# When the first MLP's narrow units are mixed into attention: a delay of 6,500 instead of 13,000 and a reserve of 54,000 instead of 60,000

## The chip, the cores and the metric

One core of one Trainium2 chip. The metric is the device time of one execution in microseconds (us); lower is better. Engines are named as in the profile: PE (TensorE matmuls), PEld (its weight loads), DVE (VectorE), ACT (ScalarE), POOL (GpSimd), SP (the queue that issues the DMAs).

## What is computed

Attention with a memory term (4 batches, 8 heads, 576 tokens, 64 wide), then two MLPs over the 2,304 tokens, all in fp32:

```python
scores = scale * q @ k.T; scores = where(causal, -1e9, scores)
a = softmax(scores); local = a @ v
q_p = phi(q)                                   # elu(q) + 1
mem_out = (q_p @ M_prev) / (q_p . z_prev + 1e-6)
x = g * mem_out + (1 - g) * local              # (2304, 512)
h = x @ w_in;  x = elu(h) @ w_out              # first MLP, d_ff 2048
h = x @ w2_in; out = leaky(h) @ w2_out         # second MLP, d_ff 2048
```

## The kernel before

**Precision.** fp32 values are split into a high and a low part (`xh`, `xl`; `gh`, `gl`; two slices of each weight tile `w`), and a product is made of three matmuls. Batch 0 of attention alone runs in plain fp32.

**Attention** (`attention_units`, up to L591) runs over 16 pairs of heads, four per batch, each of four items. An item has stages that are woven together: scores and softmax (`score`, L428 to L451), transposes of the probabilities (`tr`, L457), and the product with the values (`pv`, L524 to L532), whose result goes to DRAM (`xq_scr`, L532).

**The first MLP** has two shapes. Its first 7 of 16 slices of d_ff are computed batch by batch as **narrow units** on half a batch (288 tokens): `u_load` (L670 to L676, two loads `x` and `y` of what attention wrote), `u_x` (L682 adds the two, L610 casts to `xh` on ACT, L614 makes `xl` on POOL, for four chunks c = 0 to 3), then seven `u_h` units (12 matmuls each, L621, then ACT L633 and L634, DVE L635, the cast L241 and POOL L628), then four `u_o` units (21 matmuls each, L649, a copy L241 to `st`, a store L703 to `ys`). A batch thus has 22 units and 336 narrow matmuls. The other 9 slices and the whole second MLP follow as wide work on 512 tokens, with PE's queue full to the end.

**The order around the change** is set by a planner (L752 to L779) whose costs are planned nanoseconds, not times of the chip. `c0` is attention up to the end of batch 0 (47,290), `c_att` the rest of it (130,950), `c_mlp` all narrow units (161,280). At each attention unit of cost `c` the first MLP earns `c * rate` of credit; a narrow unit is handed out when its credit is there and `pos` is at least `DELAY` past the end of its batch:

```python
rate = (c_mlp - RESERVE) / (c_att - DELAY)
fill += [(pos + DELAY, c2, u2) for c2, u2 in more]
if fill and fill[0][0] <= pos:
    credit += c * rate
while fill and fill[0][0] <= pos and fill[0][1] <= credit:
    _, c2, u2 = fill.pop(0)
```

What is left when attention ends (`side`) is then issued ahead of the wide work, with the decoding of six weight tiles mixed in (`merge`, `load_w`, L103 to L138). The framework's scheduler takes this order as priorities and may still move single instructions on each engine; each engine's queue is executed in order. From here on the first `u_x` of batch n is called the start of batch n.

Of the kernel before, what the change touches and what calls it, by code (L numbers as in the profile page):

```python
# [24 lines left out]
def kernel(  # L25
# [36 lines left out]
    NTT = NT // TN  # L62
    NG = 7
    DSPAN = 0.75
    RESERVE = 60000.0
    EARLY = 150
    DELAY = 13000.0
    NHP = H // 2
    PSUM = bass.MemoryType.PSUM

# [686 lines left out]
    c_mlp = NFA * 24 * NT / 2.4  # L757
    rate = (c_mlp - RESERVE) / (c_att - DELAY)
    dec = [lambda f=f: load_w(0, wpa, w1i, w1o, f, f) for f in range(NFA)]
    fill = []  # L760
    credit = pos = 0.0
    for c, u, done in att:
# [7 lines left out]
        if done is not None:  # L770
            fetch, more = phase1_units(done)
            fetch()
            fill += [(pos + DELAY, c2, u2) for c2, u2 in more]
        if fill and fill[0][0] <= pos:
# [188 lines left out]
```

## Time and profile before

| | us |
|---|---|
| median of 3 runs | 1075.36 (1072.89 to 1075.43) |
| the profiled execution's own time | 1075.3 |
| its span, first to last instruction | 1073.5 |
| PE busy / PEld busy in the span | 1042.7 / 911.4 |
| DVE / ACT / POOL busy | 595.5 / 483.5 / 532.4 |

The span is cut at the places that matter: batch 0 of attention ends near 88 us, narrow matmuls begin at 124.7 us, attention's last matmul is at 394 us, and from 426 us on PE's queue is full. "Busy" of PE counts a matmul's modelled length, which overlaps the next one.

### The profile page before, as it was taken

The numbers are of one execution on the slowest core, as the hardware profiler recorded it, in microseconds if no ns is written. First come the engines' busy times: TensorE is split into PE (matmuls) and PEld (weight loads), VectorE is DVE, ScalarE is ACT, GpSimd is POOL, SyncE is SP. The second block draws the span as 40 slices with busy tenths as digits, with TensorE's granted clock in tenths as the row PEclk, the third lists the DMA queues.
The fourth block names the chain that finished last, engine by engine and source line by source line (L and its number), as shares of the span: only waits on it lengthen the run. The fifth ranks groups of instructions, "written<-read, shape, count | busy, mean of one in ns | idle before, by whom it ended". The sixth has DMA issues, their size and how long they took to land.

```text
span 1073.5 us, 17323 instructions
## 1 busy us (share of the span) xinstructions
PE 1042.7 (97%) x5904; PEld 911.4 (85%) x5904; DVE 595.5 (55%) x1382; ACT 483.5 (45%) x1169; POOL 532.4 (50%) x674
## 2 busy tenths in 40 slices
PE   7998899999998999999999999999999999999997
PEld 4776799989998998988888889888888888888896
DVE  6889987788879748576762325654322221232232
ACT  6999887778877635544442224332211211110111
POOL 7675775667657626654543225855422422222221
PEclk9999999999999999999999999999999999999999
DMA  7754544564446238765562304430200100000010
GB/s 183 197 144 116 162 137 105 124 169 144 108 121 164 89 95 286 251 227 188 191 224 66 118 1 138 157 118 1 79 1 1 64 15 1 10 30 1 1 40 20
DMA packets 150408, 115.05 MB, mean 107 GB/s; under 512 B 80048, under 2 KB 142000, under 8 KB 150320
## 3 DMA queue, kind: packets, MB, share of 16 engines
q1 hardware_dynamic: 150320, 113.94, 35.6%
q8 instruction: 47, 0.77, 0.3%
q14 instruction: 41, 0.34, 0.1%
HBM read 78.52 MB, written 31.85 MB: 103 GB/s over the span
## 4 chain that ended last, share of the span: by engine, by line
PE 87%; DVE 6%; DMA 3%; issue 1%; ACT 1%; SPq 1%; POOL 0%; DVEq 0%; ACTq 0%; POOLq 0%
PE pm L621 20%; PE tp L621 16%; PE sc L911 14%; PE sc L649 10%; PE pm L649 4%; PE po L911 4%; PE po L524 4%; PE tp L457 4%; PE po L649 3%; PE pm L524 2%; PE sc L428 1%; PE sc L426 1%; PE sc L429 1%; DVE pt L431 1%; DMA y<-xq 1%
## 5 line engine op out<-in xcount | busy, mean ns | idle before, releaser
L628 POOL TENSOR_TENSOR gl<-e,gh 128x512 fp32r<-128x512 f32 (+2 forms) x181 | 202.8, 1123 | 378.0 <-DVE gh L243 266.4
L621 PE MATMUL tp<-xw,w 128*128 128x512 f32 (+1 forms) x504 | 144.0, 367 | 0.0
L621 PE MATMUL pm<-xw,w 128*128 128x512 f32 (+1 forms) x496 | 142.1, 369 | 0.0
L911 PE MATMUL sc<-w,gh 128*128 128x512 f32 x448 | 135.9, 390 | 0.0
L451 POOL TENSOR_SCALAR pt<-pt,rs,omg 128x128 f32<-128x128 f32 (+4 forms) x160 | 102.5, 649 | 22.9 <-DVE rs L446 18.2
L649 PE MATMUL sc<-gh,w 128*128 128x512 f32 (+2 forms) x438 | 105.4, 340 | 0.3 <-DVE gh L243 0.3
L621 PEld LDWEIGHTS tp<-xw,w 128*128 128x128 f32 x504 | 91.8, 189 | 16.1
L621 PEld LDWEIGHTS pm<-xw,w 128*128 128x128 f32 x496 | 90.6, 188 | 16.1
L436 ACT ACTIVATE pt<-pt,mx 128x128 f32<-128x128 f32 (+4 forms) x160 | 93.0, 583 | 16.6 <-DVE mx L431 15.7
L911 PEld LDWEIGHTS sc<-w,gh 128*128 128x128 f32 x448 | 83.1, 188 | 16.5
L621 PE MATMUL tp<-xv,w 128*128 128x512 f32 (+1 forms) x252 | 92.5, 367 | 0.0
L621 PE MATMUL pm<-xv,w 128*128 128x512 f32 (+1 forms) x248 | 91.4, 369 | 0.0
L640 ACT ACTIVATE e<-pm 128x512 f32<-128x512 f32 (+1 forms) x40 | 22.2, 554 | 145.2 <-PE pm L621 142.2
L138 POOL TENSOR_TENSOR w<-wm,w 128x512 fp32r<-128x512 f32 x50 | 65.8, 1337 | 37.9 <-ACT w L241 37.9
L641 DVE TENSOR_TENSOR e<-tp,e 128x512 f32<-128x512 f32 (+1 forms) x40 | 25.5, 636 | 106.2 <-ACT e L640 106.2
L911 PE MATMUL sc<-w,gl 128*128 128x512 f32 x224 | 84.3, 389 | 0.0
L243 DVE CAST gh<-e 128x512 fp32r<-128x512 f32 (+2 forms) x146 | 75.4, 520 | 13.8 <-PE po L911 3.1
L649 PEld LDWEIGHTS sc<-gh,w 128*128 128x128 f32 x438 | 74.9, 188 | 9.3 <-DVE gh L243 0.6
L621 PE MATMUL pm<-xh,w 128*128 128x288 f32 x368 | 81.3, 308 | 1.5 <-ACT xh L610 1.4
L457 PE MATMUL tp<-ident,pt 128*128 128x128 f32 x480 | 80.3, 276 | 2.3 <-ACT ah L247 0.8
L641 DVE TENSOR_TENSOR e<-pm,e 128x512 f32<-128x512 f32 (+1 forms) x40 | 25.4, 636 | 102.4 <-ACT e L640 102.4
L640 ACT ACTIVATE e<-tp 128x512 f32<-128x512 f32 (+1 forms) x40 | 22.1, 552 | 117.2 <-PE tp L621 117.2
(157 smaller groups left out, 2444.7 us busy)
## 6 DMA issues: line engine op xcount, KB each, us to landing
wraw<-in_moe_w_in_dram SPq DMA_DIRECT2D x32, 512.0 KB, 3.9
wraw<-in_moe_w_out_dram SPq DMA_DIRECT2D x32, 512.0 KB, 4.7
xh<-xh SPq DMA_DIRECT2D x8, 576.0 KB, 3.1
xl<-xl SPq DMA_DIRECT2D x8, 576.0 KB, 4.1
ys<-st SPq DMA_DIRECT2D x32, 144.0 KB, 2.8
x<-x1s SPq DMA_DIRECT2D x9, 512.0 KB, 3.8
out_dram<-st SPq DMA_DIRECT2D x36, 128.0 KB, 1.7
vn<-in_v_dram SPq DMA_DIRECT2D x64, 64.0 KB, 2.3
```

Of the source, the lines that this page charges most:

```text
L138: nc.gpsimd.tensor_tensor(out=w[:, 1, a], in0=t[:, a], in1=_f(w)[:, 0, a], op=ALU.subtract)
L243: (nc.vector if eng == "V" else nc.gpsimd).tensor_copy(dst, src)
L436: nc.scalar.activation(out=pt[0:m, 0:nk], in_=pt[0:m, 0:nk], func=AF.Exp, scale=-1.0, bias=mx[0:m, last:last + 1], accum_out=self.pd["ss"] ...
L451: nc.gpsimd.tensor_scalar(out=pt, in0=pt, scalar1=rs[0:m, i:i + 1], scalar2=omg[0:m, h:h + 1], op0=ALU.mult, op1=ALU.mult,)
L457: nc.tensor.transpose(dst, self.p[c][:, k0:k0 + kn], ident)
L524: nc.tensor.matmul(po[:, a:b], w, x, start=i == 0, stop=i == len(mms) - 1)
L621: nc.tensor.matmul(ph, wi[:, wj, kc, :], xx[:, kc, :], start=n_mm == 0, stop=n_mm == 11)
L628: nc.gpsimd.tensor_tensor(out=gl, in0=g, in1=_f(gh), op=ALU.subtract)
L640: nc.scalar.mul(t, ph, 0.01)
L641: nc.vector.tensor_tensor(out=t, in0=ph, in1=t, op=ALU.max)
L649: nc.tensor.matmul(py, wo[:, wj, ec * P:(ec + 1) * P], gg, start=opens and f == first and n_mm == 0, stop=closes and f == last and n_mm == 2,)
L911: nc.tensor.matmul(pos[tb], gg[:, tb * P:(tb + 1) * P], wo[:, wj, :], start=f == 0 and n_mm == 0, stop=f == NF - 1 and n_mm == 2,)
```

## The change

Two constants of the planner; nothing else:

```diff
-    RESERVE = 60000.0
+    RESERVE = 54000.0
     EARLY = 150
-    DELAY = 13000.0
+    DELAY = 6500.0
```

`rate` goes from 0.859 to 0.862. The condition on `DELAY` holds back batch 0 alone: batches 1 and 2 become due before the last unit of the batch ahead of them is handed out, with either value. 33 units (29 now) are left over when attention ends.

ACT, at the start of batch 0 (`xh` is its cast tile, L610; L436, L342 and L249 belong to attention):

```order
190 L249 CAST ac<-tp 64x320
191 L610 CAST xh_1825<-x 128x288 x3
192 L436 ACTIVATE pt_1664,ss_157<-pt_1664,mx 128x128
193 L342 CAST qs_1586<-sc 64x320
194 L249 CAST dh_137<-tp 128x384
195 L436 ACTIVATE pt_1677,ss_157<-pt_1677,mx 128x256
```

and in the changed kernel:

```order
190 L249 CAST ac<-tp 64x320
191 L610 CAST xh_1671<-x 128x288 x3
192 L436 ACTIVATE pt_1664,ss_157<-pt_1664,mx 128x128
193 L610 CAST xh_1671<-x 128x288
194 L342 CAST qs_1586<-sc 64x320
195 L249 CAST dh_137<-tp 128x384
```

Before, the fourth cast (which every `u_h` needs) stands 27 rows behind the first three; now one row behind them. PE follows: its first narrow matmul has 387 attention matmuls ahead of it, 469 before, and 72 narrow matmuls now stand ahead of the 470th attention matmul. PE's queue there, as a difference:

```order
 L428 MATMUL sc<-kk_1538,qs_1585 128x448
 L429 MATMUL sc<-kl_1_176,qs_1585 128x448
+L621 MATMUL pm<-xh_1671,w_201 128x288 x2
+L621 MATMUL pm<-xh_1671,w_391 128x288 x2
 L524 MATMUL po<-ac,vv 128x320
 L524 MATMUL po<-dh_153,vv 128x256
```

The rest of batch 0's first units follow some 30 attention matmuls later. The stretches without narrow matmuls between two batches change too, counted in attention matmuls on PE: between batches 0 and 1 from 59 to 47, between batches 1 and 2 from 39 to 78.

PE at the end of attention (L524 is its last matmul; `gh`, `gl` are batch 2's second half), changed kernel:

```order
2008 L524 MATMUL po<-dl_139,vv 128x128
2009 L649 MATMUL sc<-gl,w_905 128x288
2010 L649 MATMUL sc<-gh,w_1010 128x288 x2
...
2028 L649 MATMUL sc<-gh,w_1010 128x288 x2
2029 L649 MATMUL sc<-gl,w_1010 128x288
2030 L621 MATMUL tp<-xh_6579,w_201 128x288 x2
2031 L621 MATMUL pm<-xh_6579,w_391 128x288 x2
2032 L621 MATMUL tp<-xh_6579,w_539 128x288 x2
2033 L621 MATMUL pm<-xh_6579,w_650 128x288 x2
```

33 narrow matmuls now stand between attention's last matmul and the first of batch 3; before there were 73. The first four `u_h` of batch 3 now run side by side in all four banks of `tp` and `pm`; before it was two. On ACT all four `st` copies of batch 2's last half now stand ahead of batch 3's casts, two before; `st` has two buffers.

## Rows read from the trace of the kernel before

**Rows 1.** Page, part 1: busy us, share of the span, instructions.
```profile
PE 1042.7 (97%) x5904; PEld 911.4 (85%) x5904; DVE 595.5 (55%) x1382; ACT 483.5 (45%) x1169; POOL 532.4 (50%) x674
```
**Rows 2.** Windows: stretch, length, busy PE, PEld, DVE, ACT, POOL (instructions); clock, DMA share, GB/s.
```profile
109.50:124.70 15.20, 12.36 (x83) 9.53 (x82) 14.92 (x47) 11.81 (x34) 11.27 (x20) 1.00 0.44 110
124.70:200.00 75.30, 75.25 (x591) 74.74 (x590) 61.49 (x187) 60.19 (x173) 52.88 (x85) 1.00 0.51 138
200.00:240.00 40.00, 36.78 (x266) 34.69 (x264) 33.56 (x104) 30.35 (x87) 26.02 (x42) 0.96 0.61 161
240.00:304.00 64.00, 64.00 (x505) 63.67 (x504) 53.79 (x162) 51.63 (x148) 45.05 (x72) 1.00 0.50 129
304.00:350.00 46.00, 41.72 (x305) 39.73 (x304) 40.04 (x118) 35.20 (x101) 32.39 (x51) 0.96 0.52 137
...
394.40:404.10 9.70, 9.70 (x75) 9.70 (x75) 2.82 (x6) 1.87 (x5) 2.10 (x4) 1.00 0.69 191
404.10:426.00 21.90, 19.59 (x143) 18.83 (x142) 17.47 (x26) 13.20 (x26) 13.18 (x14) 1.00 0.97 327
```
**Rows 3.** Timeline of ACT, batch 0's casts: start, length, engine, line, what, count.
```profile
106.38 1.10 ACT L610 CAST xh<-x 128x288 fp32r<-128x288 f32 x3
...
123.67 0.44 ACT L610 CAST xh<-x 128x288 fp32r<-128x288 f32 x1
```
**Rows 4.** Timeline of PE: the first narrow matmuls.
```profile
124.68 0.75 PE L621 MATMUL pm<-xh,w 128*128 128x288 f32 x4
```
**Rows 5.** Timeline of PE at 387 us: nine narrow matmuls lie between these two starts.
```profile
387.13 0.43 PE L621 MATMUL tp<-xh,w 128*128 128x288 f32 x2
...
388.33 0.43 PE L621 MATMUL tp<-xh,w 128*128 128x288 f32 x2
```
**Rows 6.** Timeline of ACT and of DVE: what one narrow `u_h` costs there.
```profile
127.91 0.40 ACT L633 ACTIVATE e<-pm 128x288 f32<-128x288 f32 x1
...
129.13 0.45 ACT L634 ACTIVATE e<-e 128x288 f32<-128x288 f32 x1
...
129.98 0.42 ACT L241 CAST gh<-e 128x288 fp32r<-128x288 f32 x1
...
129.28 0.45 DVE L635 SCALAR_TENSOR_TENSOR e<-e,pm 128x288 f32<-128x288 f32 x1
```
**Rows 7.** Timeline of DVE, then of PE, around the two starts of batch 2.
```profile
303.36 1.20 DVE L682 TENSOR_TENSOR x<-x,y 128x288 f32<-128x288 f32 x3 [1.38 <-DMA vn<-in_v_dram]
...
344.31 0.41 PE L524 MATMUL po<-qph,ms 128*128 128x320 f32 x1 [1.92 <-DVE xp L531]
```
**Rows 8.** Windows, PE alone: stretch, length, busy, granted clock, DMA share, GB/s.
```profile
226.00:230.00 4.00, 4.00 (x21) 0.57 0.84 321
346.00:348.00 2.00, 2.00 (x11) 0.50 0.26 59
420.00:425.00 5.00, 2.69 (x17) 1.00 0.74 268
```
**Rows 9.** Timelines of PE, DVE, SP and ACT: end of attention to batch 3's start.
```profile
393.96 0.40 PE L524 MATMUL po<-dl,vv 128*128 128x256 f32 x2
...
404.08 0.43 PE L621 MATMUL tp<-xh,w 128*128 128x288 f32 x2
...
394.39 0.49 DVE L531 COPY xp<-po 128x320 f32<-128x320 f32 x1
...
401.98 2.18 DVE L682 TENSOR_TENSOR x<-x,y 128x288 f32<-128x288 f32 x4 [6.88 <-DMA y<-xq]
...
396.73 0.52 SPq L675 DMA_DIRECT2D x<-xq  x1
...
402.47 1.17 ACT L610 CAST xh<-x 128x288 fp32r<-128x288 f32 x3 [2.83 <-DVE x L682]
```
**Rows 10.** Timeline of PE: batch 3's second half begins; line L703, 380 to 430 us: landing.
```profile
421.66 0.53 PE L621 MATMUL pm<-xh,w 128*128 128x288 f32 x2 [1.38 <-ACT xh L610]
...
DMA to landing us min/median/max: 7.0/7.6/7.9
```

## The prediction

> **What bounds the kernel now.** I read the busy times of the whole span first. PE is busy 97% of it [rows 1], so at first sight there is nothing to win for a change that only moves matmuls. That number misleads here: a matmul's modelled length covers the wait of the next one, and in the stretch before the first narrow matmul PE counts 12.36 us busy of 15.20 with 83 matmuls, while a stretch five times as long holds 591 [rows 2]. The weight loads tell more, one per matmul: where attention and narrow units are mixed they fill 74.74 of 75.30 us, in the stretch before only 9.53 of 15.20 [rows 2]. I therefore use length less PEld busy as PE's slack while attention and narrow units run. By the Trainium skill (Perfetto Trace Analysis, Identifying the Most-Contended Engine) matmul busy time is a poor measure and weight loads are one to be used; by PE busy the slack of the stretch would be 2.8 us, by the weight loads 5.7, and the counts above bear out the second.
>
> The slack lies in four places, and each is a place where no narrow matmul is ready [rows 2]: 5.67 us from 109.5 to 124.7 (attention alone, DVE busy 14.92 of 15.20), 5.31 us from 200 to 240 (batch 0 used up, batch 1 not begun), 6.27 us from 304 to 350 (the same between batches 1 and 2), and 3.07 us from 404.1 to 426 (batch 3). Between them it is 0.56 of 75.30 and 0.33 of 64.00 us. Matmuls are neither added nor taken away, so what the change is worth is what it does to these four, and to a fifth that it may open: right after attention's end, where PE is now full for 9.70 us [rows 2].
>
> **The price of a narrow matmul** is 1.20 us for nine, 0.133 us [rows 5]. A `u_h` costs ACT 0.40 + 0.45 + 0.42 = 1.27 us and DVE 0.45 us [rows 6].
>
> **1. Batch 0 begins earlier.** Before, three casts of its input are done at 106.38 and the fourth at 123.67; the first narrow matmul follows at 124.68 [rows 3, 4]. Now the fourth stands behind the third, and 72 narrow matmuls (six `u_h`), 72 x 0.133 = 9.6 us, lie among the attention matmuls that ran from 109.5 to 124.7. That stretch then needs PE 9.53 + 9.6 = 19.1 us, ACT 11.81 + 6 x 1.27 = 19.4 us and DVE 14.92 + 6 x 0.45 = 17.6 us [rows 2, 6]; DVE alone took 98% of the stretch before, so I take 19.8 us. It grows by 4.6 and does 9.6 us of work that came later: 5.0 us won. Of these I take off 0.5, since only 4 of the 72 stand in its first third. **4.5 us won**; at most the slack, 5.7, and 3.0 if the first third's slack and some of ACT's queueing stay.
>
> **2. Between batches 0 and 1** the pause shrinks from 59 attention matmuls to 47. The slack of 5.31 us is 0.09 us for each of the 59 [rows 2]; 47 make 4.2. **1.1 us won**; between 0 (the loads of batch 1's input set its start, not the order) and 2.5.
>
> **3. Between batches 1 and 2** narrow work runs out earlier, since batch 1 was handed out earlier, while batch 2 begins at the same attention matmul as before: the pause grows from 39 to 78. At 0.09 us each, 78 make 7.0 us, against 6.27 now. DVE waits 1.38 us for batch 2's input today [rows 7]; its add now stands 3 rows nearer to the last store of that batch, 3 x 0.45 = 1.4 us more of the same wait [rows 6], of which some is inside the pause already. Against it, PE's stall of 1.92 us at 344 [rows 7], when DVE stood at the next input, need not come back in another order. I take 7.4 us, **1.1 us lost**, with bounds of 2 won and 4 lost.
>
> **4. Batch 3 begins with less cover.** Its input is written by attention's last matmuls. Today: last matmul at 393.96 for two, copy at 394.39, load issued at 396.73, add at 401.98, first cast at 402.47, so a usable slice at 402.9; PE arrives at 404.08 with 73 narrow matmuls in between and does not wait [rows 9]. Now 33 stand there, 4.4 us, and PE is through at 394.3 + 4.4 = 398.7: idle until 402.9, **4.2 us lost**. Three more effects follow. First, batch 2's last two `st` copies now stand ahead of the casts on ACT, and each needs a buffer whose store must have landed. These stores took 7.6 us in this stretch, with large weight loads under way [rows 10]; now they go out ahead of the weight loads, so I take about 4.3 us, the time from the load's issue at 396.73 to its use less a margin, and 0.8 us more for the start (0 to 3.3). Second, four `u_h` run side by side, all four banks fill at the same time and the fifth waits for ACT and DVE: 0.40 + 0.45 + 0.45 us [rows 6] and the queue behind them, less the few matmuls in between, 1.0 us (0 to 2). Third, the second half of batch 3 has its own chain of loads and leaves 3.07 us of slack today, 1.38 of it one wait for the cast [rows 2, 10]; PE comes there later, so it waits less: 2.0 us back (0 to 3.07). **In sum 4.0 us lost** (1 to 9).
>
> **5. The clock.** Twice the granted clock goes to half (1.2 GHz of 2.4) for a few us, both times after a stretch with slack: 0.57 of four us at 226 and 0.50 at 346; after the waits at 420 it stays at 1.00 [rows 8]. Each costs about 4 x 0.43 = 1.7 us. Now there are three pauses that can bring it (2, 3 and 4); I leave it at two, so nothing, with 1.7 either way. The Trainium skill (TensorE: Matmul & The Clock Gate, Why this matters for your kernels) says that idle gaps of PE between bursts of matmuls bring back its lower clock; by that the new idle time of step 4, longer than any wait named above, would bring a third, 1.7 us more.
>
> **6. What costs nothing.** The six weight tiles decoded after attention have as much PE work above them as before: 48 matmuls (6.4 us) fewer, some 4 us of waiting more; from 394.4 to 404.1 DVE, ACT and POOL are busy under 3 of 9.7 us [rows 2]. The wide work is in the same order. If that cover failed, PE would wait for a tile at the first wide unit, some us at most.
>
> **Sum** against the profiled execution's 1075.3 us (the median of the runs is 1075.36): -4.5 - 1.1 + 1.1 + 4.0 = -0.5, **1074.8 us**. About 0.3%, 3.2 us, is what a measurement of this kernel can tell from no change.
>
> **Rivals.** *The early gain stays* (faster). Batch 3's second half gives back its whole 3.07 us, the first starts without the extra 0.8 and 1.0, and DVE's stall at 344 is gone: step 4 costs 1.1 and step 3 gains 0.8, and with the clock as it is -4.5 - 1.1 - 0.8 + 1.1 = -5.3, 1070.0 us. For it: the 1.92 us stall was an accident of one order. Against it: 33 matmuls cannot cover 8.5 us.
>
> *Batch 3 starts late* (slower). The place is ACT's queue after attention: its fourth `st` copy, ahead of the casts, waits for a store that lands 7.6 us after its issue, as all did there [rows 10], instead of 4.3. This puts 3.3 us more on the start, and the longer idle time brings a third stretch at half clock, 1.7: -0.5 + 3.3 + 1.7 = +4.5, 1079.8 us. It decides from a landing of about 4.5 us on; below that the loads of `x` and `y` set the start. By the clock rule cited in step 5 alone, without the late store, it would be 1076.5.
>
> *The early start does nothing*: batch 0's units are there but ACT, at 19.4 of 19.8 us, holds attention up by nearly as much as PE gains, so step 1 brings 1.0 us instead of 4.5: 1078.3 us. The mixed stretches, where ACT is busy 60.19 of 75.30 us without slack on PE [rows 2], speak against it.
>
> **How the numbers follow.** I give my forecast 0.46, the early gain 0.28, the late start 0.21 and no early gain 0.05. The range takes in the forecast's own spread (steps 3 and 4 can each be off by 2 to 3 us) and reaches to the nearer parts of both rivals: 1069.5 to 1080.5. Faster by over 0.3%: 0.28; within: 0.46; slower: 0.26.
>
> **What would show it.** Step 1: first narrow matmul near 110 us, PEld above 90% from there on, ACT busiest. Steps 2 and 3: a pause without L621 and L649 that is shorter after batch 0 and longer after batch 1. Step 4: idle time of PE of 4 to 5 us some 4.4 us after the last L524, ended by ACT's `xh`, and a wait shorter than 1.38 us at the second half. Wrong would be: no idle time there, a PE wait for `xh` ended by a `ys` store, or a change in the wide work.

## The result and the profile after

| | before | changed |
|---|---|---|
| median of 6 runs, us | 1074.21 (1072.89 to 1075.43) | 1082.76 (1079.44 to 1085.42) |
| the profiled execution's span, us | 1073.5 | 1080.6 |

The ratio is 1.0079 (95% interval 1.0065 to 1.0092). The change makes the kernel slower, by 8.55 us between the medians and by 7.1 us between the two profiled spans. The forecast was 1074.8 with a range to 1080.5, so the time is outside it.

The busy times of the whole span, which answer to [rows 1], tell nothing of this: PE is still at 97%.

```profile
PE 1044.0 (97%) x5904; PEld 915.2 (85%) x5904; DVE 588.8 (54%) x1378; ACT 483.8 (45%) x1173; POOL 528.6 (49%) x674
```

The windows do. These answer to [rows 2] and have its columns; the cuts follow the same places of the program, which now lie elsewhere in time.

```profile
109.50:124.00 14.50, 14.42 (x112) 14.01 (x111) 11.30 (x39) 10.40 (x33) 10.98 (x18) 1.00 0.63 201
124.00:196.00 72.00, 71.03 (x553) 70.13 (x554) 59.71 (x183) 58.62 (x170) 50.35 (x83) 1.00 0.42 114
196.00:240.00 44.00, 37.70 (x269) 36.47 (x268) 33.31 (x98) 31.57 (x90) 27.17 (x43) 0.92 0.59 153
240.00:300.00 60.00, 60.00 (x473) 59.62 (x473) 49.75 (x157) 47.18 (x137) 42.27 (x69) 1.00 0.45 123
300.00:342.00 42.00, 37.59 (x275) 35.47 (x274) 36.05 (x109) 32.30 (x91) 27.91 (x43) 0.96 0.68 169
...
404.80:422.00 17.20, 12.04 (x70) 11.63 (x69) 7.90 (x13) 6.68 (x15) 5.33 (x6) 0.80 1.04 325
422.00:440.00 18.00, 18.00 (x135) 17.79 (x135) 12.91 (x21) 9.88 (x21) 13.68 (x14) 1.00 0.74 232
```

Length less PEld gives the slack. At 109.5 us it is 0.49 us instead of 5.67: the early start does there what was forecast. But between batches 0 and 1 it rises to 7.53 (5.31 before) at a clock of 0.92, between batches 1 and 2 it stays at 6.53 (6.27), and from 404.8 to 422 there are 5.57 us at a clock of 0.80 where before the worst stretch had 3.07 at 1.00.

**One number per stretch.** Slack misses what the clock costs, so I also keep an account. At the start of the Nth attention matmul on PE I subtract 0.133 us [rows 5] for each narrow matmul that has run by then. N counts every attention matmul of the trace: 507 of them stand ahead of the first narrow one now and 589 before, where the section on the change counts 387 and 469; the difference of 82 is the same. Two kernels with the same account at the same N have lost equally much so far, however many narrow units each has placed. At N = 893 the kernel before starts at 200.0 us with 285 narrow matmuls done, account 162.1; the changed one at 202.6 with 332 done, account 158.5. The early start is worth 3.6 us at this point. At N = 940, only 47 attention matmuls later, the accounts are 169.1 and 169.6, and all of it is gone. At N = 1100, with batch 1 well under way in both, they are 194.1 and 194.0, at N = 1391 they are 231.4 and 235.4, and at attention's last matmul (N = 1656) 269.9 and 270.2. So attention comes out even, and the 7 us of the profiled spans are lost after it: from there to PE's last matmul 619.1 us remain before, not counting narrow matmuls, and 625.9 now.

**What happens at N = 893 to 940.** DVE reaches the adds of batch 1 before their load has landed, and waits. The same happens at batch 1's second half and at batch 2's first, three times in all (timeline of DVE, changed kernel; in brackets the idle time and what ended it):

```profile
205.68 1.20 DVE L682 TENSOR_TENSOR x<-x,y 128x288 f32<-128x288 f32 x3 [2.14 <-DMA y<-xq]
...
228.17 1.20 DVE L682 TENSOR_TENSOR x<-x,y 128x288 f32<-128x288 f32 x3 [3.14 <-DMA y<-xq]
...
309.62 1.20 DVE L682 TENSOR_TENSOR x<-x,y 128x288 f32<-128x288 f32 x3 [3.57 <-DMA y<-xq]
```

PE, which waits for an attention operation `qs` or `al` that stands behind those adds on DVE, has no narrow matmul left for the meantime (timeline of PE, changed kernel):

```profile
203.13 0.29 PE L649 MATMUL pm<-gl,w 128*128 128x288 f32 x1
...
207.90 0.39 PE L428 MATMUL sc<-kk,qs 128*128 128x256 f32 x1 [3.29 <-DVE qs L343]
...
214.61 0.69 PE L621 MATMUL pm<-xh,w 128*128 128x288 f32 x4
...
229.82 0.74 PE L457 MATMUL tp<-ident,pt 128*128 128x128 f32 x3 [3.01 <-DVE al L250]
...
311.93 0.53 PE L428 MATMUL sc<-kk,qs 128*128 128x256 f32 x1 [2.21 <-DVE qs L343]
```

The first wait is not new. In the kernel before, DVE waited 2.02 us at the same adds (timeline of DVE):

```profile
200.68 1.20 DVE L682 TENSOR_TENSOR x<-x,y 128x288 f32<-128x288 f32 x3 [2.02 <-DMA y<-xq]
```

but PE then had 51 narrow matmuls of batch 0 left, the last of them here (timeline of PE, before):

```profile
214.27 0.29 PE L649 MATMUL pm<-gl,w 128*128 128x288 f32 x1
```

Now batch 0 is used up at 203.13. The pause that follows is shorter than the one before (48 attention matmuls against 68), but its slack, length less PEld, is about as large, 3.84 us against 3.98 (windows of the changed kernel, then of the kernel before):

```profile
203.40:214.70 11.30, 8.01 (x50) 7.46 (x49) 8.63 (x27) 8.02 (x22) 5.95 (x8) 0.85 0.58 138
```

```profile
214.50:226.60 12.10, 9.75 (x70) 8.12 (x69) 11.28 (x35) 10.82 (x33) 7.65 (x15) 0.99 0.43 112
```

Before, DVE was busy for 93% of the pause; now it stands still for 2.14 us of it, and the clock is lower. The load's time belongs to attention: its second half is issued at 196.02 before and 201.24 now, behind the last store of the batch, and lands 4.6 and 4.4 us later. The Trainium skill (TensorE: Matmul & The Clock Gate, Architectural detail: the array is 16× 32×32, not 1× 128×128) says that VectorE's queue is strictly first in, first out; the trace agrees, since `qs` runs at 206.90, right behind the adds.

**The clock** falls behind each of these waits, and at the end of attention (windows, PE alone, changed kernel, columns as in [rows 8]):

```profile
208.00:214.00 6.00, 6.00 (x32) 0.72 0.38 103
228.00:234.00 6.00, 4.18 (x20) 0.72 0.48 109
310.00:316.00 6.00, 4.07 (x19) 0.72 0.47 112
406.50:414.50 8.00, 5.82 (x24) 0.57 1.01 344
```

That is 6.00 x 0.28 = 1.7 us three times and 8.00 x 0.43 = 3.4 us once, where before there were two of 1.7. Of the 3.4, 0.6 us fall in the idle time before 408.68 (the clock is 0.74 from 406.50 to there), so PE pays 2.9.

**The end of attention**, answering to [rows 9] (timelines of PE, then DVE, then ACT):

```profile
399.68 0.39 PE L524 MATMUL po<-dl,vv 128*128 128x256 f32 x2
...
408.68 0.85 PE L621 MATMUL tp<-xh,w 128*128 128x288 f32 x2 [3.69 <-ACT xh L610]
...
419.32 0.54 PE L621 MATMUL tp<-xh,w 128*128 128x288 f32 x2 [1.47 <-DVE e L635]
...
470.21 0.74 PE L621 MATMUL tp<-xw,w 128*128 128x512 f32 x2 [1.08 <-DVE e L635]
...
407.55 1.56 DVE L682 TENSOR_TENSOR x<-x,y 128x288 f32<-128x288 f32 x4 [6.95 <-DMA ys<-st]
...
407.90 0.40 ACT L241 COPY st<-sc 128x288 f32<-128x288 f32 x1 [3.77 <-DMA ys<-st]
...
408.19 1.43 ACT L610 CAST xh<-x 128x288 fp32r<-128x288 f32 x4
```

PE idles 3.69 us before batch 3, the fifth `u_h` waits 1.47 us with all four banks full, and a new wait of 1.08 us stands in the wide work at 470 us, where DVE had the decoding of a weight tile ahead of `e`. The wait of 1.38 us at the second half [rows 10] is gone. DVE's add is put down to a `ys` store; but its own `y`, issued at 403.01, took 4.3 us to land, to 407.3, just before the add, so its own load is enough to explain the wait.

### The profile page after: what moved, and what is told of

Read it like the earlier page. It is cut to its first block, busy times and chain, and to the rows that moved or that the text cites. A ratio compares the mean times of both kernels' runs of the same rounds, so it can differ in the third digit from the quotient of the medians.

```text
span 1080.6 us, 17343 instructions
## 1 busy us (share of the span) xinstructions
PE 1044.0 (97%) x5904; PEld 915.2 (85%) x5904; DVE 588.8 (54%) x1378; ACT 483.8 (45%) x1173; POOL 528.6 (49%) x674
## 4 chain that ended last, share of the span: by engine, by line
PE 85%; DMA 5%; DVE 4%; POOL 2%; ACT 2%; issue 1%; SPq 1%; DVEq 0%; POOLq 0%; ACTq 0%
PE pm L621 20%; PE tp L621 15%; PE sc L911 14%; PE sc L649 10%; PE pm L649 4%; PE po L911 4%; PE tp L457 4%; PE po L524 4%; PE po L649 3%; PE pm L524 2%; PE sc L428 1%; DMA y<-xq 1%; PE sc L429 1%; PE sc L426 1%; DMA x<-xm 1%
## 5 line engine op out<-in xcount | busy, mean ns | idle before, releaser
L451 POOL TENSOR_SCALAR pt<-pt,rs,omg 128x128 f32<-128x128 f32 (+4 forms) x160 | 100.3, 636 | 19.9 <-DVE rs L446 15.0
L436 ACT ACTIVATE pt<-pt,mx 128x128 f32<-128x128 f32 (+4 forms) x160 | 93.1, 583 | 12.6 <-DVE mx L431 11.7
L457 PE MATMUL tp<-ident,pt 128*128 128x128 f32 x480 | 82.9, 279 | 5.9 <-DVE al L250 3.0
L621 PE MATMUL pm<-xh,w 128*128 128x288 f32 x384 | 84.6, 307 | 0.0
```

The lines of the kernel that those rows point to most:

```text
L436: nc.scalar.activation(out=pt[0:m, 0:nk], in_=pt[0:m, 0:nk], func=AF.Exp, scale=-1.0, bias=mx[0:m, last:last + 1], accum_out=self.pd["ss"] ...
L451: nc.gpsimd.tensor_scalar(out=pt, in0=pt, scalar1=rs[0:m, i:i + 1], scalar2=omg[0:m, h:h + 1], op0=ALU.mult, op1=ALU.mult,)
L457: nc.tensor.transpose(dst, self.p[c][:, k0:k0 + kn], ident)
L621: nc.tensor.matmul(ph, wi[:, wj, kc, :], xx[:, kc, :], start=n_mm == 0, stop=n_mm == 11)
```

## The experiments

First the table, since the same account serves all runs. "To 893" is the account from N = 507 to 893 (the stretch of the early start), then 893 to 940 (batch 1's first adds), 940 to 1391, 1391 to attention's last matmul, and what remains from there to PE's last matmul. All come from each run's profiled execution; the ratio comes from the timed runs.

| run | ratio (95% interval) | to 893 | to 940 | to 1391 | to 1656 | after it |
|---|---|---|---|---|---|---|
| kernel before | 1 | 53.0 | 7.0 | 62.3 | 38.5 | 619.1 |
| changed kernel | 1.0079 (1.0065 to 1.0092) | 49.2 | 11.1 | 65.8 | 34.8 | 625.9 |
| e1_delay_only | 1.0080 (1.0066 to 1.0093) | 48.9 | 11.7 | 65.0 | 42.4 | 619.0 |
| e2_reserve_only | 1.0064 (1.0052 to 1.0077) | 53.0 | 7.4 | 68.6 | 37.9 | 620.6 |
| e3_delay_res66 | 1.0069 (1.0053 to 1.0084) | 49.2 | 11.7 | 62.1 | 42.1 | 622.4 |
| e4_hold | 1.0040 (1.0027 to 1.0054) | 49.6 | 11.2 | 65.7 | 38.3 | 618.2 |
| e7_end_short | 1.0044 (1.0031 to 1.0056) | 53.0 | 7.3 | 62.4 | 37.3 | 624.0 |
| e8_end_long | 1.0032 (1.0019 to 1.0045) | 49.1 | 12.2 | 67.1 | 35.6 | 621.3 |
| e9_adds_late | 1.0021 (1.0011 to 1.0031) | 49.4 | 6.8 | 63.1 | 37.7 | 625.8 |
| e10_adds_end | 0.9972 (0.9959 to 0.9985) | 51.3 | 6.7 | 63.1 | 39.0 | 618.6 |
| e11_old_adds | 0.9971 (0.9957 to 0.9985) | 53.5 | 5.8 | 59.3 | 39.6 | 618.3 |
| e12_both | 0.9965 (0.9952 to 0.9977) | 49.3 | 6.8 | 63.5 | 35.8 | 619.4 |
| e13_old_both | 0.9957 (0.9941 to 0.9973) | 53.0 | 5.8 | 59.0 | 37.1 | 618.2 |

### Each constant alone, and two other tables

`e1_delay_only` has the new DELAY with the old RESERVE:

```diff
-    DELAY = 13000.0
+    DELAY = 6500.0
```

> DELAY 6500 with the old RESERVE of 60000: batch 0 begins as early as in the changed kernel, and as many units are left for attention's end as before. Theory A (the early start is a trade: about 4.8 us are won at 109 us, and attention, which is late by as much, hands over batches 1 and 2 later, so all of it is lost again at their starts; what makes the changed kernel slower is attention's end with less cover): about 1074 us, no idle PE above 1 us between attention's end and batch 3's first matmul, PEld above 90% from 109.5 to 124 us. Rival B (the early start itself costs the 8 us, by waits of DVE for batch 1's and 2's loads and the half clock that follows; the end is a detail): 1079 to 1083 us.

`e2_reserve_only` has the new RESERVE with the old DELAY:

```diff
-    RESERVE = 60000.0
+    RESERVE = 54000.0
```

> RESERVE 54000 with the old DELAY of 13000: batch 0 begins where it did before, four units fewer are left for attention's end. Theory A: no early gain, the whole loss at the end (idle PE of 4 us before batch 3, the half clock after it, four full banks, a wait in the wide part): 1074.2 + 5 to 7 = 1079 to 1081 us. Rival B: the order before attention's end is the old one in kind, so within 2 us of the kernel before, 1073 to 1076 us.

They took 1083.07 and 1081.93 us (the kernel before, timed beside them, 1075.01). So each constant alone costs nearly what both cost together, which neither theory had: B comes near with e1 and A with e2, but A had put e1 at 1074, and B had put e2 at 1073 to 1076. The table shows where. e1 wins 4 us on the way to 893, loses 4.7 there, and another 2.7 and 3.9 later in attention, with its end untouched; e2 loses 6.3 us between 940 and 1391. Counted on PE, the two pauses without narrow matmuls are 122 and 114 attention matmuls in e1 and 111 and 122 in e2, against 68 and 39 in the kernel before (I had counted 59 for the first). Each constant reorders all that follows, so one constant alone is not one part of the change. Windows of the first pause in e1, then its adds on DVE:

```profile
203.20:229.60 26.40, 18.98 (x124) 16.23 (x123) 22.59 (x73) 18.89 (x55) 13.83 (x24) 0.94 0.54 127
```

```profile
207.18 1.20 DVE L682 TENSOR_TENSOR x<-x,y 128x288 f32<-128x288 f32 x3 [3.04 <-issue]
...
228.37 0.45 DVE L682 TENSOR_TENSOR x<-x,y 128x288 f32<-128x288 f32 x1
```

That is 10.2 us of slack against 4.0 in the kernel before (window above). Batch 1's first narrow matmul has 1012 attention matmuls ahead of it in both, while batch 0 ends earlier in e1. Its load does not hold it there: three adds are done by 208.4, and the fourth, which every `u_h` needs, stands 20 us behind them on DVE.

`e3_delay_res66` spreads the narrow units thinner:

```diff
-    RESERVE = 60000.0
+    RESERVE = 66000.0
...
-    DELAY = 13000.0
+    DELAY = 6500.0
```

> DELAY 6500 and RESERVE 66000: early start of batch 0, narrow units thinner, about 14 more units' matmuls (101) left for attention's end than in the changed kernel. Theory A: attention's end without any idle time (as before, 0), but pauses of 92 and 142 attention matmuls against 59 and 39 before, (234 - 98) x 0.09 = 12 us lost against 4.8 won: about 1081 us. Rival B (loads late against early starts): the starts come later, after their loads, so 1070 to 1074 us.

1082.42 us, near theory A's number, but not shown to come from longer pauses: 4.7 us more than before go at batch 1's adds, and 3.3 us more after attention, where PE waits 2.76 us in the wide work, at 470 us. `e4_hold` hands batches 1 and 2 out later, on top of the changed kernel:

```diff
-            fill += [(pos + DELAY, c2, u2) for c2, u2 in more]
+            fill += [(pos + (DELAY, 15300.0, 17800.0, 0.0)[done], c2, u2) for c2, u2 in more]
```

> The changed kernel (RESERVE 54000, batch 0 after 6500), but batches 1 and 2 are handed out no earlier than 15300 and 17800 past the end of their batch, about where the kernel before had them, so their loads have landed when DVE comes to the adds. The pause between batches 0 and 1 grows from 48 to 103 attention matmuls, that between 1 and 2 shrinks from 78 to 52; about two more units are left for the end. Theory A with the wait of DVE for the loads as its means: the two waits of 2 to 3 us of DVE at batch 1's starts go, with the PE stalls of 3.3 to 3.6 us and one stretch at half clock, but the longer pause costs 0.09 us for each of 55 matmuls, 5 us: 1080 to 1083 us, no better than the changed kernel. Rival C (the waits and the half clock are what matters, an attention matmul alone costs nothing if no wait is behind it): 1075 to 1077 us.

1078.93 us, between the two theories, and not a test of the wait: the scheduler left the three adds of batch 1 where they were, DVE waited 2.15 us at 205.93 as before, and 11.2 us went between 893 and 940. What it won over the changed kernel it won after attention, where 63 narrow matmuls stand behind the last attention matmul instead of 33 (618.2 against 625.9).

### The end alone

`e7_end_short` is the kernel before with a short end, `e8_end_long` the changed kernel with the old end:

```diff
-            credit += c * rate
+            credit += c * (rate if pos < 154250.0 else 1.3)
```

```diff
-            credit += c * rate
+            credit += c * (rate if pos < 147550.0 else 0.675)
```

> The kernel before up to batch 2 (its matmuls are in the same order up to the 1298th of attention), then batch 2's units handed out faster, so that 37 narrow matmuls instead of 74 lie behind attention's last one, about the changed kernel's 33. Theory D (the loss of the changed kernel is the end: short cover, idle PE, half clock, all banks full, a wait in the wide part; what happens up to attention's end nets out at zero): 1075 + 5 to 7 = 1080 to 1082 us, with 3 to 4 us of idle PE before batch 3's first matmul. Rival E (the end costs little by itself, since work that lies in attention's stretches of slack comes free; the loss is in attention): 1074 to 1077 us.

> The changed kernel up to batch 2 (same order of matmuls up to the 1355th of attention), then batch 2's units handed out more slowly, so that 74 narrow matmuls lie behind attention's end, as in the kernel before. Theory D: the changed kernel's 1082.8 less 5 to 7, 1075 to 1078 us, no idle PE above 1.7 us after attention. Rival E: 1080 to 1083 us, the same loss before attention's end.

1079.75 and 1078.71 us, beside 1075.51 of the kernel before. e7 is 0.0044 x 1075 = 4.7 us above the kernel before, e8 is (1.0079 - 1.0032) x 1075 = 5.1 us below the changed kernel. The end is worth some 5 us from either side, at the lower edge of what theory D gave, and it is not the whole loss: e8 is still 3.4 us above the kernel before, so D's "nets out at zero" for attention falls. The end of e7 shows the waits of the changed kernel again (timeline of PE):

```profile
398.13 0.40 PE L524 MATMUL po<-dl,vv 128*128 128x256 f32 x2
...
406.99 0.81 PE L621 MATMUL tp<-xh,w 128*128 128x288 f32 x2 [3.49 <-ACT xh L610]
...
416.60 0.53 PE L621 MATMUL tp<-xh,w 128*128 128x288 f32 x2 [1.47 <-DVE e L635]
```

e8's profiled execution (1082.85 us) lies 4.1 us above its median, so its row of the table is read for the places, not for the sum.

### The wait for batch 1's load

`e9_adds_late` holds the first halves' adds of batches 1 and 2 behind the score that was issued last (a queue order on DVE, no semaphore); `e10_adds_end` adds the edit of `e8_end_long`:

```diff
-                nc.vector.tensor_tensor_reduce(
+                pools["dve"] = nc.vector.tensor_tensor_reduce(
...
-                )
+                ).ins
...
-        units = [(0, lambda: u_x(*mine[0]))]
+        def u_x0():
+            with tc.issue_after(pools["dve"]):
+                u_x(*mine[0])
+
+        units = [(0, u_x0 if ti in (1, 2) else lambda: u_x(*mine[0]))]
```

> The changed kernel, with the four adds of each of the first halves of batches 1 and 2 held on DVE behind the scores that the planner issues ahead of them (row 515 of DVE's queue instead of 500 for batch 1). Theory F (the early gain is lost because DVE, in order, stands at batch 1's adds from 203.5 to 205.7 us until their loads land, while PE has no narrow matmul left, and the clock drops behind it): the stall of PE of 3.6 us at 204 us goes, with the stretch at half clock at 209 us: 3 to 5 us off 1082.8, 1078 to 1080 us. Rival G (attention alone runs at the speed of DVE and ACT there, so the wait is only moved into other stalls): 1081 to 1083 us.

> Both: the adds held as in the run with late adds, and batch 2's units handed out more slowly, so that about 100 narrow matmuls lie behind attention's end. Theories D and F together: 1082.8 less 5 to 7 less 3 to 5, 1071 to 1075 us, which would be faster than the kernel before by up to 3 us. Rivals E and G: 1080 or more.

1077.25 and 1072.46 us. e9 is (1.0079 - 1.0021) x 1075 = 6.2 us below the changed kernel, a little more than theory F gave (its profiled execution is the slowest of its runs, 2.1 us above the median). DVE now comes to the adds at 209.34 and waits for nothing, and the clock stays up at both places (timeline of DVE, then windows of PE alone, of e9):

```profile
209.34 1.73 DVE L682 TENSOR_TENSOR x<-x,y 128x288 f32<-128x288 f32 x4
```

```profile
208.00:214.00 6.00, 5.58 (x40) 1.00 0.53 131
228.00:234.00 6.00, 5.81 (x39) 1.00 0.30 76
```

893 to 940 takes 6.8 us instead of 11.1. Every run of the table with the early start and the adds where the scheduler put them takes 11.1 to 12.2 us there, every other one 5.8 to 7.4. The wait at 228 us shrank with it: DVE's at the second half is 1.10 us in e9, 3.14 in the changed kernel. What is left in e9 is the changed kernel's end, and a wait of PE of 2.34 us at 329.86 that the changed kernel does not have. e10 shows that the two losses add up: 5.1 + 6.2 = 11.3 us expected below the changed kernel, (1.0079 - 0.9972) x 1075 = 11.5 measured, with 99 narrow matmuls behind attention's end where e8 has 74. It is faster than the kernel before by 0.28%.

### Is the early start worth anything?

`e11_old_adds` has the old start with late adds; its edit in the loop fixes the score behind which they stand at 9 us of planned time past the batch's end:

```diff
+        for n, e in ends.items():
+            if pos >= e + 9070.0:
+                ref.setdefault(n, pools["dve"])
         if done is not None:
+            ends[done] = pos
```

> The kernel before (DELAY 13000, RESERVE 60000) with the first halves' adds of batches 1 and 2 held on DVE behind a score that lies 9 us of planned time past the end of the batch, which puts batch 1's at row 515 as in the runs with late adds; about 100 narrow matmuls are left behind attention's end, as in the run with adds and end. It tells what the early start is worth once DVE no longer waits. Theory H (the early start is worth its 3 to 4.5 us there): 1075 to 1077 us, 3 to 4.5 us above the 1072.5 of the run with adds and end. Rival I (the late adds alone make that run faster; the early start is worth nothing): 1071 to 1073 us.

1070.83 us, ratio 0.9971 against e10's 0.9972: rival I. Late adds alone take 3.1 us off the kernel before (0.0029 x 1075; about 25 more narrow matmuls behind attention's end are in that too), and the early start adds nothing that can be seen: the two ratios differ by 0.0001, with some 0.002 (2 us) of uncertainty.

e10 had a wait of PE left at batch 2's second half (timelines of PE, then DVE, then SP, of e10):

```profile
330.85 0.39 PE L428 MATMUL sc<-kk,qs 128*128 128x320 f32 x1 [2.66 <-DMA kk<-kk]
...
330.64 1.79 DVE L682 TENSOR_TENSOR x<-x,y 128x288 f32<-128x288 f32 x3 [1.37 <-DMA kk<-kk]
...
323.18 1.99 SPq L675 DMA_DIRECT2D x<-xq  x2
325.21 1.33 SPq L301 DMA_DIRECT2D kk<-kk  x2
```

I took it for another wait behind the adds. The rows do not say that: PE waits for attention's own `kk`, which was issued right behind the batch's loads and took up to 5.5 us to land, and its wait began 1.1 us before DVE's.

`e12_both` holds the second halves' adds too, and `e13_old_both` does the same to e11 (74 narrow matmuls lie behind attention's end in e12, 99 in e13):

```diff
-                    units.append((0, lambda k=k: u_x(*mine[k + 1])))
+                    units.append((0, lambda k=k: (u_x0(k + 1) if ti in (1, 2) else u_x(*mine[k + 1]))))
```

> The run with adds and end, and the second halves' adds of batches 1 and 2 held in the same way (batch 2's at row 831 of DVE's queue instead of 815). In that run DVE waits for batch 2's second half from 328 to 330.5 us, with a PE stall of 2.96 us at 327.9 and a stretch at half clock at 331.8. Theory F: both go, 3 to 4 us off 1072.5: 1068 to 1070 us, faster than both kernels. Rival G (the wait only moves): 1072 to 1074 us.

> The run with the old start and late adds, and the second halves' adds of batches 1 and 2 held as well, as in the run with both halves; it differs from that run by the start of batch 0 (DELAY 13000 here, 6500 there) and by 25 narrow matmuls more behind attention's end. Theory H again (the early start is worth 3 us or more once no add waits for its load): 1073 to 1075 us, a ratio to the kernel before of 0.999 to 1.001, against 0.9965 there. Rival I (what is won at 109 us is lost again at the later pauses, since narrow work that is done early is missing there, wait or no wait): within 1 us of the run with both halves, 1069 to 1071 us, ratio 0.996 to 0.998.

1069.90 us (before 1074.20) and 1070.22 us (before 1075.36). The stall at 328 us is gone from e12, but of the 3 to 4 us off 1072.5 only 2.6 came, and by the ratios (0.9972 and 0.9965) the intervals overlap: a small gain that these runs don't prove. e13 has the old start: 0.9957, against 0.9965 with the early one, intervals overlapping, so rival I's times again. Windows of e12, then of e13, columns as above:

```profile
109.50:124.00 14.50, 14.15 (x111) 13.76 (x110) 11.02 (x39) 10.26 (x32) 10.88 (x19) 1.00 0.63 200
196.00:240.00 44.00, 42.11 (x312) 39.16 (x312) 40.09 (x121) 36.51 (x105) 32.92 (x49) 1.00 0.65 170
300.00:342.00 42.00, 36.21 (x276) 34.41 (x275) 38.69 (x110) 33.00 (x98) 30.09 (x48) 1.00 0.64 157
388.00:430.00 42.00, 39.59 (x291) 38.52 (x290) 25.39 (x36) 19.55 (x41) 24.43 (x23) 1.00 0.77 244
```

```profile
109.50:124.70 15.20, 12.55 (x81) 9.48 (x80) 14.89 (x48) 12.11 (x37) 12.47 (x22) 1.00 0.45 117
196.00:240.00 44.00, 42.28 (x326) 40.86 (x326) 38.91 (x118) 35.65 (x103) 31.71 (x52) 1.00 0.65 166
300.00:342.00 42.00, 40.25 (x307) 38.64 (x306) 37.29 (x115) 34.52 (x98) 29.61 (x48) 1.00 0.62 159
388.00:430.00 42.00, 40.26 (x299) 39.58 (x298) 26.73 (x40) 22.05 (x45) 26.55 (x26) 1.00 0.89 293
```

The slack of e12 is 0.7, 4.8, 7.6 and 3.5 us, that of e13 5.7, 3.1, 3.4 and 2.4: 5.0 us won by the early start and 1.7 + 4.2 + 1.1 = 7.0 lost later. Over attention as a whole (507 to 1656) their accounts are 155.4 and 154.9. But most of the 4.2 us is one wait that has nothing to do with narrow work running out: PE stands still for 2.88 us until 341.81, since DVE spends 3.56 us on one small operation of attention (timeline of DVE, of e12):

```profile
337.83 3.56 DVE L393 SCALAR_TENSOR_TENSOR den<-den,ging 128x10 f32<-128x10 f32 x1
```

The median of this operation is 0.17 us. Counted from N = 507, e12 is still 1.6 us ahead of e13 at N = 1480, and 1.6 behind at N = 1500, on the other side of this wait. So these pairs show that the early start brought nothing, and not that it must: another order may keep some of its gain.

e13 and e12 are the fastest kernels here, 0.43% and 0.35% below the kernel before, 1.2% and 1.1% below the changed one; nothing tells them apart.

## Why the prediction was wrong

The numbers are accounts of the profiled execution, predicted against measured.

- **Step 1, 4.5 us won**: 3.6 measured at N = 893. Right in mechanism and nearly in size: slack 0.49 us, first narrow matmul at 109.5, PEld at 97%.
- **Step 2, "1.1 us won"**: this is the step that failed. 4.1 us lost between N = 893 and 940. I priced the pause at 0.09 us for each attention matmul, as if its slack came from the matmuls, and so took a shorter pause for a cheaper one. It did get shorter (from 68 matmuls to 48; I had counted 59 and 47), but its slack stayed near 4 us, since the pause moved to where DVE waits for a load whose time attention sets. What made that wait cheap before was batch 0's narrow work, which ran until 214 us; the early start used up that cover ahead of the wait. I had even named the case, as the lower bound of the step ("the loads of batch 1's input set its start, not the order"), and given it a price of 0. DVE's wait of 2.02 us at 200.68 was in the trace of before; I read only its sister of 1.38 us at 303 [rows 7]. e9 shows the step: without that wait, 893 to 940 takes 6.8 us again (batch 2's first adds are held there too).
- **Step 3, 1.1 lost**: -0.2 by the account, in two larger parts: 3.9 us lost between N = 1310 and 1391, in the pause, where DVE waited 3.57 us for batch 2's load, and 3.7 won back by attention's end, where the stall of 1.92 us at 344 and its clock are gone. The sum was near, by luck. The stall itself I had misread: DVE did not stand at the next input there, but took 4.12 us for three adds that take 1.20 elsewhere (timeline of DVE, before):

```profile
339.80 4.12 DVE L682 TENSOR_TENSOR x<-x,y 128x288 f32<-128x288 f32 x3 [1.24 <-DMA xq<-xp]
```

- **Step 4, 4.0 lost**: the idle time (forecast 4.2, measured 3.69) and the four full banks (1.0 and 1.47) came as described, the 0.8 for a later start did not, and the wait at the second half went, as counted on; e7 and e8 put the whole end at 4.7 and 5.1 us. In the profiled execution of the changed kernel it is 6.8, of which up to 2.9 is the clock, that step 5 had left out.
- **Step 5, no change of the clock**: wrong. Four drops where there had been two, the last of double length, 4.6 us more in sum. They are no further cause but part of the losses above. By the rule of the Trainium skill quoted in that step (TensorE: Matmul & The Clock Gate, Why this matters for your kernels) idle gaps of PE between bursts of matmuls bring back the lower clock; the four windows above agree, each behind a wait of 2.21 to 3.69 us, and one wait of e12 does not (last section).
- **Step 6, nothing**: nearly. One new wait of 1.08 us in the wide work, at 470 us.

Of the rivals, *the early gain stays* is refuted by the account at N = 940. *The early start does nothing* had the right effect for a wrong reason: ACT did not hold attention up. *Batch 3 starts late* had a right consequence (one more drop of the clock) from a mechanism that hardly counted: the fourth `st` copy did wait for its store, but the load was no earlier.

A larger error stands behind the list. I added up four stretches as if each could change alone. The early start is worth 3.6 us where it acts, but with waits as they are it costs 3.4 us in the end (e8), or 8.6 in another order (e1), and with the waits removed it changes nothing that can be seen (e10 against e11, e12 against e13). Where the gain goes is shown for the changed kernel by e9. Why it goes in e10 and e12 is open: narrow units that ran early are missing at the later pauses, but each of the two also has a wait of PE with a cause of its own (e10 at 331 us for `kk`, e12 at 342 us behind the slow operation on DVE). Left open is how the end's 5 us divide between the idle time, the clock and the full banks, since no run changes one of them alone.

## What to carry to other kernels

Filler work that covers one wait is not free to be used earlier: before moving it, ask what it covers where it stands, and read the in-order engines for waits that hide there. Where an engine in the main path must take in a late load for the filler, queue that operation behind enough main-path work for the load to land; here this was worth 3 us in the old order (a longer end is in that too) and 6 in the new one, while the two tuned constants won nothing. Compare two orders by an account at the same point of the main work, not by the pauses one by one.

## What was not expected of the hardware

The clock does not follow a single wait's length. After waits of 2.2 to 3.7 us in the changed kernel it fell each time, but in e12 PE waited 2.88 us and the clock stayed at 1.00 (timeline of PE, then windows of PE alone, of e12):

```profile
341.81 0.53 PE L621 MATMUL pm<-xh,w 128*128 128x288 f32 x2 [2.88 <-DVE e L635]
```

```profile
341.00:347.00 6.00, 5.20 (x41) 1.00 0.13 36
```

And in the kernel before it fell at 226 us [rows 8] at the end of a pause of attention alone, in which no wait of PE was longer than this one (timeline of PE, before):

```profile
223.81 0.33 PE L428 MATMUL sc<-kk,qs 128*128 128x128 f32 x1 [0.83 <-DVE qs L343]
```

So in these runs a drop came behind most such waits, but not behind all, and it came without one too: it can't be booked as certain either way.

An operation on DVE can take many times its usual time: 3.56 us instead of 0.17 in e12, 4.12 instead of 1.20 in the kernel before (both shown above). In both cases POOL worked without a break meanwhile (in e12 until 341.4 us, where DVE's operation ends; in the kernel before until 343.6, where DVE's ends at 343.9). These runs do not show that this is the cause.
